# Fused attention and two-layer MoE kernel: the eight one-head products of each weight pair kept together, in a batch's last eight steps

## The chip, the cores and the metric

The kernel runs on one core of one Trainium2 chip. The metric is the device time in microseconds of one execution; lower is better. Inputs and output are float32.

## What is computed

Three stages follow one another, for 8 batches of 576 tokens and 8 heads of 64 columns.

```python
def sm_attn(qq, kk, vv):
    s = scale * np.matmul(qq, kk.transpose(0, 1, 3, 2))
    a = softmax(s)                       # per row
    return np.matmul(a, vv)
p_packed = sm_attn(p, k, v)              # 32 packed rows per batch and head ("pp")
out = sm_attn(q, p_packed, p_packed)     # attention of 576 tokens to 32 rows
x = out.transpose(0, 2, 1, 3).reshape(B * S, H * D)
h = x @ w_in                             # 512 -> 2048
x = (s * np.maximum(h, 0) ** 2 + b) @ w_out
a, b = x @ w1, x @ w2
return (a * b @ w3) @ w_out2
```

## The kernel before, in words

The kernel never forms the attention output. Since `x @ w_in` is (weights of the second softmax) times (pp w_in), it computes for each batch and head the 32 by 512 products **pp w_in** and multiplies them with the 256 by 576 softmax weights `AT` of the batch. Most products run in three passes of a high and a low part (`mm3`, lines 85 to 90): low weights by high data, high by low, high by high.

The work up to about 91 us (the first phase) computes pp of the first four batches (units of four heads: `A_tr`, `B_s1`, `C_tr`, `D_mm`, `D_ev`), decodes `w_in` from 64-bit words into `winx`, stores it to DRAM as `win_d`, and starts decoding `w_out`. The second phase is a loop over 256 steps (line 989 on): 8 batches by 2 halves of 288 tokens by 16 blocks of 128 columns of `w_in`. Step `idx` runs `step_h(idx + 3)` (6 products into `hps`: pp w_in by `AT`), whose result goes through ReLU and squares on ScalarE (ACT) and VectorE (DVE) to `gh` and `gl`, and `step_x(idx)` (12 products into the four banks `xps`: `w_out` by `gh`, `gl`). Beside them, by step numbers written in tables, run: the token tiles of a coming batch (`plan_q`: transpose `qtp`, scores `scp`, softmax, transpose `atp`; five per batch), the remaining units of pp (`plan`, which puts them into steps with room in the two banks of tag `a2`), the weight pairs described next, and decoding of later weights. The last phase (from about 900 us) is the second MoE.

**A weight pair** (`W_pair`, lines 498 to 518) makes pp w_in for two heads of an even batch and two of the odd batch after it, 512 columns wide. It is eight products (two heads `i`, two batches `bb`, two row halves `r`) of a 64-row by 32-column weight, each in a place of its own in the 128 by 128 array. The four with `bb = 0` fill one PSUM bank, `ps[0]`, the other four the second, `ps[1]`. Bank 0 is then read by an ACT cast (`wph`) and a DVE subtraction (`wpl`, which needs `wph`), bank 1 by an ACT copy (`wpst`). Both banks are the two buffers of tag `a2`, which token tiles and units also use. Their name in the profile is `wps`.

There are 32 pairs. The eight of batches 0 and 1 run in the first phase, in other banks. The other 24 run in the second phase, eight during each of batches 1, 3 and 5, for the two batches that follow. Their steps within the batch are `WAT`, those of the loads of their two pieces of `win_d` are `WLD` (two DMAs of 256 KB each into a ring of six buffers `wl`, so three pairs fit):

```python
WAT = (19, 20, 24, 25, 27, 28, 30, 31)
WLD = (13, 14, 16, 20, 21, 25, 26, 28)
```

Two pairs give the weights of four steps `step_h` of the next batch. All DMAs are issued by SyncE's queue (SP) in one order.

The order on each engine is not that of the code alone: a scheduler places an instruction when it expects its inputs to be ready, except where `tc.keep_in_program_order` holds those marked to the order of the code among themselves. The products of `W_pair` are marked in the first phase alone, and there those of bank 1 alone (`if bp == 0 and bb`).

Of the kernel before, what the change touches and what calls it, by code (L numbers as in the profile page):

```python
# [22 lines left out]
def fused_kernel(  # L23
# [24 lines left out]
    nc = tc.nc  # L48
    B, H, S, D = q.shape
    NP = p.shape[2]  # L50
# [13 lines left out]
    FB1 = F1 // P  # L64
# [55 lines left out]
    ppT = ppp.tile([P, NBP, NPAIR, 2, 2 * NP], F32, tag="ppT", name="ppT", bufs=1)  # L120
# [44 lines left out]
    if True:  # L165
# [332 lines left out]
        def W_pair(bp, j, ps, src):  # L498

            fc, c = divmod(j, 2)  # L500
            for i in range(2):
                for bb in range(2):
                    for r in range(2):
                        rows = slice(D * r, D * (r + 1))
                        o = NP * (r ^ bb)
                        h = 64 * (i ^ bb) + o
                        ins = nc.tensor.matmul(  # L507
                            ps[bb][h:h + NP], ppT[rows, bp, 2 * c + i, bb, o:o + NP], src[i][rows],
                            start=True, stop=True,
                        )  # L510
                        if bp == 0 and bb:
                            tc.keep_in_program_order(ins)
            if c == 0:
                wch[2 * bp, fc] = wch_tiles()
                wst[2 * bp + 1, fc] = wch_p.tile([P, 2, FC], F32, tag="wpst", name="wpst", bufs=4)
            hi, lo = wch[2 * bp, fc]
            split(hi[:, c], lo[:, c], ps[0])
            nc.scalar.copy(wst[2 * bp + 1, fc][:, c], ps[1])
# [8 lines left out]
        wd, wx = {}, {}  # L527
# [33 lines left out]
        ps = ps0.tile([P, 512], F32, tag="w", name="warm", bufs=2)  # L561
# [108 lines left out]
        ps = ps0.tile([P, 2, 512], F32, tag="s1", name="warm")[:, 0]  # L670
# [15 lines left out]
        def a2_ps(name):  # L686
            return psh.tile([P, 512], F32, tag="a2", name=name, bufs=2)
# [3 lines left out]
        def plan_q(b, j, o):  # L691

            def act(step, fn, first=False):
                l_ = qact.setdefault(step, [])
                l_.insert(0, fn) if first else l_.append(fn)

            qload.setdefault(max(o - 10, 0), []).append((b, j))
            act(o, lambda: q_tr(b, j, a2_ps("qtp")))
            act(o + 1, lambda: q_sc(b, j, a2_ps("scp")))
            act(o + 2, lambda: q_sm1(b, j))  # L700
            act(o + 3, lambda: q_sm2(b, j))
            act(o + 4, lambda: box.__setitem__((b, j), q_at(b, j, a2_ps("atp"))))
            act(o + 5, lambda: q_ev(b, j, box.pop((b, j))), True)
            a2use.update((o, o + 1, o + 4))
# [4 lines left out]
            plan_q(1, j, 12 + 5 * j)  # L709
        for b in range(2, B):  # L710
            for j in range(NTILE):
                plan_q(b, j, 2 * FB1 * (b - 1) + 2 + 5 * j)

        gt = {}

        def step_h(idx):
            b, f = divmod(idx, 2 * FB1)
            hf, f = divmod(f, FB1)
            fc, fo = divmod(f, FC // P)
            wh, wl = wch[b, fc]  # L720
            ah, al = AT[b, hf]
            ws = slice(fo * P, (fo + 1) * P)
            ps = psh.tile([P, 512], F32, tag="h", name="hps", bufs=2)
            for kc in range(2):
                mm3(ps[:, :HS], wh[:, kc, ws], wl[:, kc, ws],
                    ah[:, kc, :], al[:, kc, :], kc == 0, kc == 1)
            r = ap.tile([P, HS], F32, tag="r", name="r", bufs=3)
            nc.scalar.activation(r, ps[:, :HS], AF.Relu)  # L728
            gh = ap.tile([P, HS + 2], F32R, tag="gh", name="gh", bufs=4)
            gl = ap.tile([P, HS + 2], F32R, tag="gl", name="gl", bufs=4)  # L730
            if idx < FB1:
                nc.gpsimd.memset(gh[:, HS:].bitcast(F32), 1.0)
                nc.gpsimd.memset(gl[:, HS:].bitcast(F32), 0.0)
            by_act = idx % 2 or idx < FB1
            if by_act:
                nc.scalar.activation(gh[:, :HS], r, AF.Square)
            nc.scalar.activation(r, r, AF.Square)  # L737
            if not by_act:
                nc.vector.tensor_copy(gh[:, :HS], r)
            nc.vector.tensor_tensor(  # L740
                out=gl[:, :HS], in0=r, in1=gh[:, :HS].bitcast(F32), op=ALU.subtract
            )
            gt[idx] = (gh, gl)
# [3 lines left out]
        def step_x(idx):  # L747
            n, r = divmod(idx, 2 * FB1)
            b = n
            hf, f = divmod(r, FB1)  # L750
            gh, gl = gt.pop(idx)
            w = HS + 2 if idx < FB1 else HS
            for ob in range(KD):
                if f == 0:
                    xps[ob] = psh.tile([P, 512], F32, tag=f"x{ob}", name="xps")
                os_ = slice(ob * P, (ob + 1) * P)
                mm3(xps[ob][:, :w], wo_t[f][:, 0, os_], wo_t[f][:, 1, os_],
                    gh[:, :w], gl[:, :w], f == 0, f == FB1 - 1)
            if f == FB1 - 1:
                st = ap.tile([P, KD, HS], F32, tag="xst", name="xst", bufs=1)  # L760
                for ob in range(KD):
                    bc = bcol[:, ob:ob + 1]
                    if idx < FB1:
                        nc.vector.tensor_scalar_mul(bc, xps[ob][:, HS:HS + 1], sb_b[:, 0:1])
                    if ob % 2 == 0:
                        nc.scalar.activation(
                            st[:, ob, :], xps[ob][:, :HS], AF.Identity, bias=bc, scale=sb_s[:, 0:1]
                        )
                    else:
                        nc.vector.tensor_scalar(  # L770
                            out=st[:, ob, :], in0=xps[ob][:, :HS], scalar1=sb_s[:, 0:1],
                            scalar2=bc, op0=ALU.mult, op1=ALU.add,
                        )
                nc.sync.dma_start(
                    out=x2_d[b][hf].rearrange("(o p) t -> p o t", p=P), in_=st
                )
# [72 lines left out]
        NST = B * 2 * FB1  # L849
        for idx in range(3):  # L850
            step_h(idx)
        WAT = (19, 20, 24, 25, 27, 28, 30, 31)
        WLD = (13, 14, 16, 20, 21, 25, 26, 28)
        JOB0 = 66
        PRE = NST - 24

# [141 lines left out]
        for idx in range(NST):  # L998
            n, r = divmod(idx, 2 * FB1)
            if idx + AHEAD < FB1:  # L1000
                wo_dec(idx + AHEAD)
            if idx + AHEAD + 4 < FB1:
                wo_load(idx + AHEAD + 4)
            if idx == LATE:
                ctxl.close()
                ctxl.enter_context(ExitStack())
                p3["S"] = ctxl.enter_context(pool("ss"))
            nn, k = divmod(idx, 2 * FB1)
            if nn % 2 == 1 and nn + 1 < B:
                for j in range(len(WAT)):  # L1010
                    if k == WLD[j]:
                        W_load(j)
                    if k == WAT[j]:
                        W_pair((nn + 1) // 2, j, [a2_ps("wps") for _ in range(2)], wx.pop(j))
            nn, k = divmod(idx - 20, 2 * FB1)
            if nn >= 0 and nn % 2 == 0 and k in (0, 4, 8, 12):
                split_wp(nn + 1, k // 4)
            for fn in qact.pop(idx, ()):
                fn()
            for bj in qload.pop(idx, ()):  # L1020
                if bj[0]:
                    load_q(*bj)
            for fn in late.pop(idx, ()):
                fn()
            if idx >= JOB0:
                n, ph = divmod(idx - JOB0, 4)
                if ph and later:
                    later.pop(0)()
                if ph == 0:
                    job(n, 0)  # L1030
                    job(n - 2, 3)
                elif ph == 2:
                    job(n - 1, 1)
                elif ph == 3:
                    job(n - 1, 2)
            if idx + 3 < NST:
                step_h(idx + 3)
            step_x(idx)
            if PRE <= idx < PRE + 2 * FB2 and (idx - PRE) % 2 == 0:
                load_wo2((idx - PRE) // 2)  # L1040
            if PRE + 3 <= idx < PRE + 3 + 2 * FB2 and (idx - PRE) % 2 == 1:
                split_wo2((idx - PRE - 3) // 2)
            if idx in (NST - 12, NST - 8):
                load_w3(VM[(idx - NST + 12) // 4])
            if idx == NST - 3:
                V_tr(VM[0], a2_ps)
# [307 lines left out]
        j = NB3 - 1  # L1354
# [71 lines left out]
```

## Time and profile before

| | |
|---|---|
| time, three runs | 1446.88, 1448.70, 1449.66 us (median 1448.7) |
| profiled execution: time / span | 1446.5 / 1444.7 us |
| PE (TensorE) busy | 1424.6 us, 99% of the span |
| DVE / ACT busy | 851.2 us, 59% / 701.1 us, 49% |
| chain that ended last | 94% PE |
| all pairs' products: `wps` | 512 records, of 256 products |

The span is 1.8 us shorter than the execution's own time. A float32 product stands in the trace as two records (two passes), so a pair's eight products are 16 records, and one bank's four are 8. Products overlap, so their durations don't add up: what a group costs is read from the starts of its neighbours.

### The profile page before, as it was taken

What the parts mean: (1) busy time and instruction counts of PE and PEld (TensorE: products, weight loads), DVE (VectorE), ACT (ScalarE), POOL (GpSimd) and SP (SyncE); (2) the same over time, 40 slices, a digit from 0 to 9 for tenths busy, and PEclk for the clock granted to TensorE, in tenths of its full rate; (3) what the DMA queues carried; (4) which work ended last, traced back from release to release, by engine and by line L of the source; (5) the groups of instructions that cost most, each with busy time, mean ns of one, the idle gap of its engine ahead of it and who ended that gap; (6) DMA issues with size and microseconds to landing.
All of it is one profiled execution on the core that took longest, in us unless ns stands there. A gap on an engine that the chain in (4) does not pass through costs nothing.

```text
span 1444.7 us, 29157 instructions
## 1 busy us (share of the span) xinstructions
PE 1424.6 (99%) x11545; PEld 1314.6 (91%) x11545; DVE 851.2 (59%) x1686; ACT 701.1 (49%) x1509; POOL 4.2 (0%) x40
## 2 busy tenths in 40 slices
PE   8999999999999999999999999999999999999997
PEld 6569999699997799987999998999999999999997
DVE  5877544345644456665687337476685766757556
ACT  4777555455565556555676434142242433324323
POOL 0000000000000000000000000000000000000000
PEclk9999999999999999999999999999999999999999
DMA  8974220242433543445544143776675856757551
GB/s 287 342 276 136 64 65 26 94 141 66 147 110 102 188 122 112 124 157 166 160 163 154 55 143 111 237 237 180 191 232 156 264 164 196 226 165 215 160 162 44
DMA packets 177575, 228.93 MB, mean 158 GB/s; under 512 B 55584, under 2 KB 109856, under 8 KB 177440
## 3 DMA queue, kind: packets, MB, share of 16 engines
q1 hardware_dynamic: 177440, 227.08, 51.6%
q8 instruction: 92, 1.51, 0.4%
q14 instruction: 43, 0.35, 0.1%
HBM read 182.98 MB, written 44.04 MB: 157 GB/s over the span
## 4 chain that ended last, share of the span: by engine, by line
PE 94%; DMA 2%; DVE 2%; ACT 1%; issue 0%; SPq 0%; ACTq 0%
PE xps L89 10%; PE xps L90 10%; PE xps L86 10%; PE prod L86 8%; PE prod L90 7%; PE prod L89 7%; PE hps L86 5%; PE hps L90 5%; PE hps L89 5%; PE yps L89 4%; PE yps L90 4%; PE yps L86 4%; PE wps L507 3%; PE scp L201 2%; PE qtp L187 1%; PE w4a L86 1%
## 5 line engine op out<-in xcount | busy, mean ns | idle before, releaser
L89 PE MATMUL xps<-gl,wo 128*128 128x288 f32 (+1 forms) x1024 | 305.4, 299 | 0.0
L90 PE MATMUL xps<-gh,wo 128*128 128x288 f32 (+1 forms) x1024 | 304.8, 299 | 0.0
L86 PE MATMUL xps<-gh,wo 128*128 128x288 f32 (+1 forms) x1024 | 302.3, 299 | 0.0
L86 PE MATMUL prod<-xc,whl 128*128 128x384 f32 x672 | 226.3, 337 | 2.8 <-ACT Ta L1066 1.8
L90 PE MATMUL prod<-xc,whl 128*128 128x384 f32 x672 | 225.0, 335 | 0.0
L89 PE MATMUL prod<-xc,whl 128*128 128x384 f32 x672 | 224.9, 335 | 0.0
L86 PEld LDWEIGHTS xps<-gh,wo 128*128 128x128 f32 x1024 | 191.7, 188 | 10.4 <-issue 9.3
L90 PEld LDWEIGHTS xps<-gh,wo 128*128 128x128 f32 x1024 | 192.5, 188 | 9.4 <-issue 8.9
L89 PEld LDWEIGHTS xps<-gl,wo 128*128 128x128 f32 x1024 | 192.7, 188 | 8.3 <-issue 7.3
L740 DVE TENSOR_TENSOR gl<-r,gh 128x288 fp32r<-128x288 f32 x256 | 116.4, 455 | 126.7 <-ACT r L737 122.7
L728 ACT ACTIVATE r<-hps 128x288 f32<-128x288 f32 x256 | 105.2, 411 | 156.6 <-PE hps L90 155.0
L86 PE MATMUL hps<-ATh,wpl 128*128 128x288 f32 x512 | 154.5, 302 | 0.0
L89 PE MATMUL hps<-ATl,wph 128*128 128x288 f32 x512 | 152.8, 298 | 0.0
L90 PE MATMUL hps<-ATh,wph 128*128 128x288 f32 x512 | 152.3, 298 | 0.0
L1066 ACT COPY Ta<-prod 128x384 f32<-128x384 f32 x96 | 46.1, 480 | 215.5 <-PE prod L90 214.7
L90 PE MATMUL yps<-w4c,op 128*128 128x256 f32 x504 | 142.2, 282 | 0.0
L89 PE MATMUL yps<-w4c,op 128*128 128x256 f32 x504 | 142.1, 282 | 0.0
L86 PE MATMUL yps<-w4c,op 128*128 128x256 f32 x504 | 140.9, 280 | 0.0
L86 PEld LDWEIGHTS prod<-xc,whl 128*128 128x128 f32 x672 | 126.2, 188 | 7.3 <-ACT Ta L1066 3.8
L89 PEld LDWEIGHTS prod<-xc,whl 128*128 128x128 f32 x672 | 126.2, 188 | 0.0
L90 PEld LDWEIGHTS prod<-xc,whl 128*128 128x128 f32 x672 | 126.1, 188 | 0.0
L737 ACT ACTIVATE r<-r 128x288 f32<-128x288 f32 x256 | 112.8, 444 | 5.6
(161 smaller groups left out, 2378.5 us busy)
## 6 DMA issues: line engine op xcount, KB each, us to landing
whl<-whl SPq DMA_DIRECT2D x336, 256.0 KB, 3.1
raw<-in_moe_w_dram SPq DMA_DIRECT2D x32, 512.0 KB, 4.5
raw<-in_moe_w_out_dram SPq DMA_DIRECT2D x24, 512.0 KB, 4.4
wl<-win SPq DMA_DIRECT2D x48, 256.0 KB, 3.1
q<-in_q_dram SPq DMA_DIRECT2D x72, 128.0 KB, 3.6
x<-xst SPq DMA_DIRECT2D x16, 576.0 KB, 3.3
out_dram<-O SPq DMA_DIRECT2D x72, 128.0 KB, 2.4
raw<-in_moe_w_in_dram SPq DMA_DIRECT2D x16, 512.0 KB, 6.1
```

The source lines that it names most:

```text
L86: ins = nc.tensor.matmul(ps, wl, xh, start=start, stop=False, **kw)
L89: nc.tensor.matmul(ps, wh, xl, start=False, stop=False, **kw)
L90: nc.tensor.matmul(ps, wh, xh, start=False, stop=stop, **kw)
L187: nc.tensor.transpose(ps[:, pr * P:pr * P + n], src[:n, 2 * pr:2 * pr + 2, :].rearrange("p h d -> p (h d)"), ident[:n, :n],)
L201: nc.tensor.matmul(ps[sl, c:c + 64], qT[b, t][:, pr, sl], ppT[:, b // 2, pr, b % 2, :], start=True, stop=True,)
L507: ins = nc.tensor.matmul(ps[bb][h:h + NP], ppT[rows, bp, 2 * c + i, bb, o:o + NP], src[i][rows], start=True, stop=True,)
L728: nc.scalar.activation(r, ps[:, :HS], AF.Relu)
L737: nc.scalar.activation(r, r, AF.Square)
L740: nc.vector.tensor_tensor(out=gl[:, :HS], in0=r, in1=gh[:, :HS].bitcast(F32), op=ALU.subtract)
L1066: tc.keep_in_program_order(nc.scalar.copy(out, src))
```

## The change

In `W_pair` all eight products are marked to keep their order, bank 0's four before bank 1's, and ahead of them stands a new product of the same weight and data as the last of the eight, two columns wide, into bank 1 (the eight write over it). Pairs stand in steps 24 to 31 of the batch, after `step_h` of their step; their loads move to later steps; and the token tiles of batches 2, 4 and 6 stand every four steps instead of every five.

```diff
         def W_pair(bp, j, ps, src):
             fc, c = divmod(j, 2)
-            for i in range(2):
-                for bb in range(2):
+            ins = nc.tensor.matmul(
+                ps[1][:NP, :2], ppT[D:, bp, 2 * c + 1, 1, :NP], src[1][D:, :2], start=True, stop=True
+            )
+            tc.keep_in_program_order(ins)
+            for bb in range(2):
+                for i in range(2):
                     for r in range(2):
...
-                        if bp == 0 and bb:
-                            tc.keep_in_program_order(ins)
+                        tc.keep_in_program_order(ins)
...
-                plan_q(b, j, 2 * FB1 * (b - 1) + 2 + 5 * j)
+                plan_q(b, j, 2 * FB1 * (b - 1) + 2 + (4 if b % 2 == 0 else 5) * j)
...
-        WAT = (19, 20, 24, 25, 27, 28, 30, 31)
-        WLD = (13, 14, 16, 20, 21, 25, 26, 28)
+        WAT = (24, 25, 26, 27, 28, 29, 30, 31)
+        WLD = (20, 21, 22, 25, 26, 27, 28, 29)
...
-                    if k == WAT[j]:
-                        W_pair((nn + 1) // 2, j, [a2_ps("wps") for _ in range(2)], wx.pop(j))
...
             if idx + 3 < NST:
                 step_h(idx + 3)
+            for nn in range(1, B - 1, 2):
+                j = idx - 2 * FB1 * nn
+                if j in WAT:
+                    j = WAT.index(j)
+                    W_pair((nn + 1) // 2, j, [a2_ps("wps") for _ in range(2)], wx.pop(j))
             step_x(idx)
```

Three places show how the order on PE moves. A row is an instruction, or several alike; `32x512` is the output, and `[waits ...]` names the semaphores that it waits for (`DMAHW` a load, `Activation` ACT). First, PE near the end of batch 1, before: the sixth of the eight pairs.

```order
L89 MATMUL hps<-ATl,wph 128x288
L90 MATMUL hps<-ATh,wph 128x288
L507 MATMUL wps<-wl,ppT 32x512 [waits DMAHW4_49,DVE_49]
L507 MATMUL wps<-wl,ppT 32x512
L507 MATMUL wps<-wl,ppT 32x512 [waits DMAHW5_49]
L507 MATMUL wps<-wl,ppT 32x512
L86 MATMUL hps<-ATh,wpl 128x288
L89 MATMUL hps<-ATl,wph 128x288
L507 MATMUL wps<-wl,ppT 32x512 [waits Activation_49]
L507 MATMUL wps<-wl,ppT 32x512 x3
L90 MATMUL hps<-ATh,wph 128x288
```

The sixth pair of the same batch in the changed kernel:

```order
L86 MATMUL xps<-gh,wo_1485 128x288
L89 MATMUL xps<-gl,wo_1485 128x288
L90 MATMUL xps<-gh,wo_1485 128x288
L501 MATMUL wps<-wl,ppT 32x2 [waits DMAHW3_49,DVE_49]
L511 MATMUL wps<-wl,ppT 32x512 [waits DMAHW2_49,Activation_49]
L511 MATMUL wps<-wl,ppT 32x512 x7
L86 MATMUL hps<-ATh,wpl 128x288 [waits Activation_49]
L89 MATMUL hps<-ATl,wph 128x288
```

Four products, two of `hps`, four products have become the two-column product and eight in a row. Over the second phase the pairs stood in 44 separate groups (40 of four products, 4 of eight) and now stand in 24 groups of eight; in 18 of them the two-column product stands directly ahead of the eight, in 6 it stands alone among `xps` or `hps` products.

Second, PE at the change from batch 1 to batch 2 in the changed kernel: the second and third pair.

```order
L511 MATMUL wps<-wl,ppT 32x512 x7
L501 MATMUL wps<-wl,ppT 32x2 [waits DVE_49]
L86 MATMUL hps<-ATh,wpl 128x288
L89 MATMUL hps<-ATl,wph 128x288 [waits Activation_49]
L90 MATMUL hps<-ATh,wph 128x288
L86 MATMUL hps<-ATh,wpl 128x288
L89 MATMUL hps<-ATl,wph 128x288
L90 MATMUL hps<-ATh,wph 128x288
L511 MATMUL wps<-wl,ppT 32x512 [waits Activation_49]
L511 MATMUL wps<-wl,ppT 32x512 x7
```

The third pair's two-column product now stands right behind the second pair's eight, and the eight of the third six products later. In this batch the first pair stands in the 64th of the 256 steps of `xps`, the last in the 71st; before, they stood from the 54th to the 66th.

Third, PE a little earlier in the changed kernel: the two-column product of the first pair of batch 1.

```order
L483 MATMUL ppp<-swap,pvx 128x128 [waits DVE_49]
L90 MATMUL xps<-gh,wo_1935 128x288
L86 MATMUL xps<-gh,wo_1935 128x288
L501 MATMUL wps<-wl,ppT 32x2 [waits DVE_49]
L89 MATMUL xps<-gl,wo_1935 128x288
L90 MATMUL xps<-gh,wo_1935 128x288
```

It stands alone, 20 products ahead of its eight.

## Rows read from the trace of the kernel before

**Rows 1.** Page, part 1: busy time of each engine

```profile
PE 1424.6 (99%) x11545; PEld 1314.6 (91%) x11545; DVE 851.2 (59%) x1686; ACT 701.1 (49%) x1509; POOL 4.2 (0%) x40
```

**Rows 2.** Waits of PE from 240 to 700 us: total, times, longest

```profile
PE atp L235 <- DVE wpl L81: 0.3, 1, 0.3
```

**Rows 3.** Timeline of PE, half a pair (start, duration, line, tiles, records)

```profile
252.75 0.29 PE L86 MATMUL hps<-ATh,wpl 128*128 128x288 f32 x1
...
253.42 0.29 PE L90 MATMUL xps<-gh,wo 128*128 128x288 f32 x1
253.64 1.06 PE L507 MATMUL wps<-wl,ppT 64*32 64x512 f32 x8
254.63 0.40 PE L86 MATMUL xps<-gh,wo 128*128 128x288 f32 x1
254.87 0.29 PE L89 MATMUL xps<-gl,wo 128*128 128x288 f32 x1
```

**Rows 4.** Timeline of PE, first half pair of phase two, behind a token tile's scores

```profile
249.17 0.69 PE L201 MATMUL scp<-ppT,qT 128*64 128x64 f32 x16
249.78 1.06 PE L507 MATMUL wps<-wl,ppT 64*32 64x512 f32 x8
250.77 0.40 PE L89 MATMUL xps<-gl,wo 128*128 128x288 f32 x1
251.01 0.29 PE L90 MATMUL xps<-gh,wo 128*128 128x288 f32 x1
```

**Rows 5.** Timeline of PE, last half pair

```profile
683.81 1.06 PE L507 MATMUL wps<-wl,ppT 64*32 64x512 f32 x8
```

**Rows 6.** Timeline of PE, a pair whose eight products stood together

```profile
291.81 0.29 PE L90 MATMUL hps<-ATh,wph 128*128 128x288 f32 x1
292.04 1.09 PE L507 MATMUL wps<-wl,ppT 64*32 64x512 f32 x16
293.05 0.40 PE L86 MATMUL hps<-ATh,wpl 128*128 128x288 f32 x1
293.30 0.29 PE L89 MATMUL hps<-ATl,wph 128*128 128x288 f32 x1
```

**Rows 7.** Timeline of PE, a token tile's scores

```profile
97.16 0.69 PE L201 MATMUL scp<-ppT,qT 128*64 128x64 f32 x16
97.77 0.40 PE L89 MATMUL xps<-gl,wo 128*128 128x290 f32 x1
```

**Rows 8.** Timeline of PE, a single product of a pair in the first phase

```profile
59.23 1.04 PE L507 MATMUL wps<-winx,ppT 64*32 64x512 f32 x2
60.20 0.44 PE L235 MATMUL atp<-ident,E 128*128 128x128 f32 x2
```

**Rows 9.** Timelines of PE, ACT and DVE, a pair and its evictions

```profile
296.43 1.09 PE L507 MATMUL wps<-wl,ppT 64*32 64x512 f32 x16
...
297.62 0.59 ACT L78 CAST wph<-wps 128x512 fp32r<-128x512 f32 x1 [0.99 <-PE wps L507]
298.10 0.59 ACT L518 COPY wpst<-wps 128x512 f32<-128x512 f32 x1
...
298.24 0.69 DVE L81 TENSOR_TENSOR wpl<-wps,wph 128x512 fp32r<-128x512 f32 x1 [0.77 <-ACT wph L78]
```

**Rows 10.** Windows, pairs of batch 5: us, PE, PEld, DVE, ACT, POOL, PEclk, DMA, GB/s

```profile
639.00:691.00 52.00, 52.00 (x386) 36.29 (x387) 31.75 (x72) 30.82 (x67) 0.00 (x0) 1.00 0.53 161
```

**Rows 11.** Chain that ended last, 74 to 92 us: start, us, what

```profile
76.13 6.67 DMA raw<-in_moe_w_out_dram
...
82.81 4.17 DMA wl<-win
...
90.75 0.46 PE ppp L483 x2
```

**Rows 12.** Waits of SyncE's queue: total, times, longest

```profile
SPq L847 <- PE wps L507: 99.0, 18, 20.3
```

**Rows 13.** Page, part 6: the loads of the pairs, count, size, us to landing

```profile
wl<-win SPq DMA_DIRECT2D x48, 256.0 KB, 3.1
```

More of the change, by code (lines that the diff above doesn't have):

```diff
@@ L1007, in fused_kernel @@
                 p3["S"] = ctxl.enter_context(pool("ss"))
-            nn, k = divmod(idx, 2 * FB1)
-            if nn % 2 == 1 and nn + 1 < B:
+            for nn in range(1, B - 1, 2):
                 for j in range(len(WAT)):
+                    k = idx - 2 * FB1 * nn
                     if k == WLD[j]:
                         W_load(j)
-                    if k == WAT[j]:
-                        W_pair((nn + 1) // 2, j, [a2_ps("wps") for _ in range(2)], wx.pop(j))
             nn, k = divmod(idx - 20, 2 * FB1)
@@ L1037, in fused_kernel @@
                 step_h(idx + 3)
+            for nn in range(1, B - 1, 2):
+                j = idx - 2 * FB1 * nn
+                if j in WAT:
+                    j = WAT.index(j)
+                    W_pair((nn + 1) // 2, j, [a2_ps("wps") for _ in range(2)], wx.pop(j))
             step_x(idx)
```

## The prediction, made before the changed kernel was run

> **What bounds the kernel now.** I read the page first: PE is busy for 1424.6 of 1444.7 us [rows 1], and the chain that ended last is 94% PE. Then the waits of PE alone, in the stretch where the 24 moved pairs lie: from 240 to 700 us it waited once, for 0.3 us [rows 2]. So there the time is the sum of what PE's instructions take in their order, and nothing that only shortens a wait elsewhere can help. What the busy share hides stands in the timeline: products of a pair hold up the stream around them. In steady work a 128-row product starts every 0.134 us (five starts from 252.75 to 253.42, [rows 3]). A group of four products of a pair (8 records) starts 0.22 us after the last product before it, the next product starts 0.99 us later, and the one after that 0.24 us later [rows 3]: 1.45 us where two starts would take 0.27, so **1.18 us for half a pair**. When all eight stood together (16 records), the same three steps took 0.23, 1.01 and 0.25 us [rows 6]: 1.49 less 0.27, **1.22 us for a whole pair**. Second, and less visible, is that the price does not depend on the number of products: one alone held the array 0.97 us [rows 8], four 0.99, eight 1.01. Eight products in eight places run side by side, so breaking a pair in two buys a second fixed price.
>
> **What merging saves.** In the second phase of before there are 40 groups of four and 4 of eight, the first half pair at 249.78 [rows 4], the last at 683.81 [rows 5]. Of the 40, 36 stand among 128-row products: 36 x 1.18 = 42.5 us. Four stand right behind a token tile's scores. Scores end 0.61 us after their start with or without a pair behind them [rows 4, 7], so the way in is shared, and such a half adds 0.99 us: 4.0 us. The 4 whole ones add 4 x 1.22 = 4.9. Together 51.4 us. The changed order has 24 groups of eight, none beside scores: 24 x 1.22 = 29.3 us. **The gross gain is 22.1 us.**
>
> **What the two-column product costs.** No row shows it. In 18 groups it stands directly ahead of the eight, in the same array shape. Below, it is free, as one product took no less than eight. Above, it costs two records as dense as those of scores: 16 records in 0.61 us [rows 7], in two halves of the array, 8 behind each other, so 0.076 us each and 0.15 for two. The first passes of its neighbours go to other places, so I take 0.1: 1.8 us (0 to 2.7). In 6 groups it stands alone among 128-row products and adds a change of shape in and out. Below: the two edges of rows 3, 0.22 + 0.24 - 0.27 = 0.19, and two records, 0.34. Above: a whole tile of scores, 0.61 + 0.19 = 0.80. It is far nearer the first; I take 0.4: 2.4 us (2.0 to 4.8). So 17.9 us remain.
>
> **The new waits.** Before, each half waited for one bank. Now the two-column product waits for one bank, at the head of PE's queue, and the eight for the other; behind them stands everything. When is the second bank free? With a pair starting at 296.43, the cast runs at 297.62, the copy at 298.10, the subtraction from 298.24 to 298.93 [rows 9]: 2.50 us after the start. PE itself is through after 1.02 us. In the order shown with the change, most pairs have 14 or more products between them, so PE comes again after 1.02 + 0.24 + 13 x 0.134 = 3.0 us at the earliest, and does not wait. Three gaps of batches 1 and 3 are shorter. The third pair of batch 1 stands directly behind the second: 2.50 - 1.02 = 1.5 us. The second stands 9 products behind the first: 1.02 + 0.24 + 8 x 0.134 = 2.3, so 0.2 us. Batch 3 has 12 products in one gap: 2.7, no wait. I take **1.7 us of new waits**; from 0 (the weights of step 64 of `hps` wait for the same evictions anyway, but other work could have covered it) to 5 (every gap of batches 1, 3 and 5 at a batch's end late by 1 us, as ACT and DVE, busy 59% and 61% of the densest such stretch [rows 10], have other work ahead of an eviction).
>
> **Loads, tiles and queues.** The 48 loads are the same. Three pairs fit the ring, so loads of the fourth pair on wait for the pair three ahead, and SyncE's queue stands behind them: 99.0 us in 18 waits before [rows 12]. The loads now go out closer to their use, so I expect less of that. A load lands 3.1 us after its issue [rows 13], two steps take over 5 us (36 products at 0.134 and a pair or two), so it is there in time. What waits behind them in the queue, token tiles and the units' k and v, is used a few steps later. I cost this at nothing; without that cover a late load costs at most its own 3.1 us less the way to it. Tiles every four steps change no count: scores, transposes and unit products are as many, and groups of other shapes differ by one or two (within 0.5 us either way). POOL has nothing there.
>
> **The first phase.** Its eight pairs also close up, but I cost that at nothing. Its end hangs on DMA and decoding: the chain runs from 76.13 through a load of `w_out` and a store of `win` to 86.98, then through ACT and DVE to a product at 90.75 [rows 11]. PE time saved before that only waits longer. If that cover were thinner the gain is at most about 3 us; a worse order on DVE may cost 2.
>
> **The sum.** 22.1 - 1.8 - 2.4 - 1.7 = 16.2 us. The profiled execution took 1446.5 us, so 1430.3; the median of three lies 2.2 above it, so **1432 us** (1448.7 - 16.2 = 1432.5). With all bounds at their best, 22.1 - 2.0 + 3 = 23.1 gain: 1426. At their worst, 22.1 - 2.7 - 4.8 - 5 - 2 - 0.5 = 7.1: 1442.
>
> **The rivals.**
> Rival A, PE gains in the first phase too. For it: PE is nearly full there as well. Against: rows 11. 3 us more: 1429.
> Rival B, the evictions are late at the batch ends and half of the gain turns into waits at PE's head. For it: `hps` of the next batch needs the first two pairs, which now come ten steps later, in the 64th step instead of the 54th; in the order shown, `xps` of batch 1 run out there. Against: the 2.50 us. 8 us of wait: 1440.
> Rival C, slower: PE runs ahead of ACT, so that every one of the 24 pairs finds its bank taken. Such a wait per pair eats the gain at 17.9 / 24 = 0.75 us, and is slower by over 2.9 us from 0.87 us on. It decides where ACT's cast stands behind a ReLU whose `hps` products stand after the pair: one step (3.6 us) later the bank is free at 6.1 us, while PE, with 24 products between, comes at 4.3; 1.8 x 24 = 43 us less 18: 1474. For it: ACT works strictly in the order it was given. Against: in rows 9 ACT stood idle for 0.99 us waiting for the pair.
> Rival D, that merged products do not run side by side, since two of a bank's four come from the lower rows of the array and two from the upper, into one bank. If they took turns, a pair would hold PE twice 0.99, and 24 pairs would cost 24 x 2.2 = 53 us: no gain, with the two-column products about 1454. Against: rows 3 and 6 show such groups at 0.99 and 1.01. The Trainium skill (TensorEngine Tiling (Array Packing), Restrictions and Gotchas) says that different row tiles cannot access the same PSUM bank simultaneously, which would be this case; the 1.01 us row speaks against it. The change could also fail to do what it says, but on PE's own order the eight stand together in all 24 pairs.
>
> **How the numbers follow.** I give the forecast 0.74, A 0.10, B 0.08, C 0.05, D 0.03. A measurement of this kernel can tell about 0.2% (2.9 us) from no change. The forecast, A and nearly all of B are faster by over 0.2%: 0.90. A part of B and C where the waits just cancel the gain gives 0.04 for within 0.2%; the rest of C and D 0.06 for slower. The range is 1425 to 1442: it holds the forecast with its bounds, A, and B; what it leaves out is C, D and surprises.
>
> **What would show it.** Right: in the second phase `wps` in 24 groups, each 18 records (16 where the two-column product stands apart), the next product about 1.0 to 1.1 us after the start; batches 1, 3 and 5 each 5 to 6 us shorter, the other stretches unchanged; PE's waits of 1 to 2 us at the end of batch 1; phase one's end still near 91 us. Wrong: a pair that holds PE for 2 us (D); waits of PE for ACT or DVE evictions at most pairs (C) or of several us in one place (B); a wait of PE for `wl` loads.

## The result, and the profile after

| | before | changed |
|---|---|---|
| median of four runs each | 1448.99 us (1446.88 to 1449.66) | 1426.85 us (1425.45 to 1428.25) |
| profiled execution: time / span | 1446.5 / 1444.7 us | 1425.45 / 1423.3 us |

The ratio is 0.985, with a 95% interval of 0.9833 to 0.9867: 22.1 us less, where 16.2 were forecast. The time lies inside the range, near its low end.

The page's busy times, which answer to [rows 1]: PE is busy for 27 us less, VectorE (DVE) as long as before.

```profile
PE 1397.4 (98%) x11609; PEld 1312.4 (92%) x11609; DVE 851.3 (60%) x1686; ACT 696.9 (49%) x1509; POOL 3.9 (0%) x40
```

First, the second phase. The waits of PE from 240 to 700 us in the changed kernel (total, times, longest) answer to [rows 2], which had 0.3 us:

```profile
PE wps L501 <- DVE wpl L81: 1.4, 1, 1.4
PE wps L501 <- ACT wpst L521: 0.4, 1, 0.4
```

So PE is still the bound there. Its timeline (start, duration, line, tiles, records), at a pair with the two-column product (L501) directly ahead of the eight (L511), answers to [rows 6]:

```profile
286.32 0.29 PE L86 MATMUL xps<-gh,wo 128*128 128x288 f32 x1
286.55 0.19 PE L501 MATMUL wps<-wl,ppT 64*32 64x2 f32 x1
286.55 0.65 PE L511 MATMUL wps<-wl,ppT 64*32 64x512 f32 x7
286.60 0.17 PE L501 MATMUL wps<-wl,ppT 64*32 64x2 f32 x1
286.63 1.02 PE L511 MATMUL wps<-wl,ppT 64*32 64x512 f32 x9
287.58 0.40 PE L86 MATMUL hps<-ATh,wpl 128*128 128x288 f32 x1
287.82 0.30 PE L89 MATMUL hps<-ATl,wph 128*128 128x288 f32 x1
```

Eighteen records stand together, and the next product starts 1.03 us after the first of them; in [rows 6], with sixteen, it was 1.01. The first records of the eight start with those of the two-column product, not behind them, so it costs **0.02 us**. In the trace of the second phase 17 of the 24 pairs look like this.

Where the two-column product stands alone among 128-row products (the first pair of batch 1):

```profile
271.53 0.29 PE L86 MATMUL xps<-gh,wo 128*128 128x288 f32 x1
271.75 0.22 PE L501 MATMUL wps<-wl,ppT 64*32 64x2 f32 x2
271.90 0.40 PE L89 MATMUL xps<-gl,wo 128*128 128x288 f32 x1
272.14 0.29 PE L90 MATMUL xps<-gh,wo 128*128 128x288 f32 x1
```

The three steps take 0.22, 0.15 and 0.24 us: 0.61, less the 0.27 of two starts, **0.34 us**. At the change from batch 1 to batch 2, the second pair, with the third pair's two-column product directly behind it:

```profile
278.16 0.29 PE L90 MATMUL hps<-ATh,wph 128*128 128x288 f32 x1
278.38 1.09 PE L511 MATMUL wps<-wl,ppT 64*32 64x512 f32 x16
280.88 0.22 PE L501 MATMUL wps<-wl,ppT 64*32 64x2 f32 x2 [1.41 <-DVE wpl L81]
281.03 0.40 PE L86 MATMUL hps<-ATh,wpl 128*128 128x288 f32 x1
```

And what it waits for, on ACT and DVE (in brackets the engine's idle time before, and what ended it):

```profile
279.51 0.59 ACT L78 CAST wph<-wps 128x512 fp32r<-128x512 f32 x1 [2.05 <-PE wps L511]
279.99 0.59 ACT L521 COPY wpst<-wps 128x512 f32<-128x512 f32 x1
...
280.13 0.69 DVE L81 TENSOR_TENSOR wpl<-wps,wph 128x512 fp32r<-128x512 f32 x1 [1.97 <-ACT wph L78]
```

The bank is free 2.50 us after the pair's start, the same as in [rows 9], and the wait is **1.4 us**. One more, of 0.4, stands at the seventh pair of batch 5 (675.00). The pair before it started at 670.00 and 25 products stand between, but ACT had other work ahead of the evictions:

```profile
673.88 0.58 ACT L78 CAST wph<-wps 128x512 fp32r<-128x512 f32 x1
674.36 0.59 ACT L521 COPY wpst<-wps 128x512 f32<-128x512 f32 x1
```

So the bank came free 4.95 us after the pair's start there, and not 2.50. From the first `hps` product to the last `xps` the second phase took 756.5 us before (92.90 to 849.37) and takes 738.6 now (89.36 to 827.92): **17.9 us less**.

SyncE's queue stands less behind the pairs, as forecast (99.0 us in [rows 12]); the loads still land in 3.1 us, as in [rows 13]. Its waits:

```profile
SPq L850 <- PE wps L511: 75.3, 18, 23.6
```

Second, the first phase. Up to the third `ppp` product of a unit's end PE's order is the same in both kernels (585 records in the trace); behind it the eight pairs begin, in the old form ahead of the fourth `ppp` and in the new one after it. Before, the third starts at

```profile
51.03 0.49 PE L483 MATMUL ppp<-swap,pvx 128*128 128x128 f32 x2
```

and the eighth at 90.75 [rows 11], 39.7 us later; now they start at

```profile
49.57 0.49 PE L483 MATMUL ppp<-swap,pvx 128*128 128x128 f32 x2
...
87.19 0.49 PE L483 MATMUL ppp<-swap,pvx 128*128 128x128 f32 x2 [2.38 <-DVE pvx L472]
```

37.6 us apart: **2.1 us less**. The stretch also starts 1.5 us earlier, though the order up to there is the same; more on that below. 17.9 + 2.1 + 1.5 = 21.5, against 21.4 us by which the span is shorter.

The chain that ended last no longer runs through DMA there, as [rows 11] did, but through evictions of pairs and products (start, us, what):

```profile
75.38 0.48 ACT wph L78
75.86 0.50 ACT wpst L521
76.36 0.04 issue
76.40 0.33 PE ppp L485
76.73 0.12 PE wps L501
76.85 0.93 PE wps L511 x10
```

Windows of the stretch from the third to the eighth `ppp` product (us, PE, PEld, DVE, ACT, POOL, PEclk, DMA share, GB/s), before:

```profile
51.03:90.75 39.72, 36.73 (x750) 19.83 (x749) 31.90 (x80) 27.98 (x65) 0.38 (x8) 1.00 1.03 360
```

and in the changed kernel:

```profile
49.57:87.19 37.62, 31.47 (x767) 20.50 (x765) 32.57 (x81) 28.45 (x66) 0.38 (x8) 1.00 1.06 365
```

PE is 5.3 us less busy, and the stretch is 2.1 us shorter: the other 3.2 us have become waiting of PE. DVE, ACT and the DMA engines do much the same as before.

### The profile page after: what moved, and what is told of

It is laid out like the page before. It is cut to its first block, busy times and chain, and to the rows that moved or that the text cites. A ratio compares the mean times of both kernels' runs of the same rounds, so it can differ in the third digit from the quotient of the medians.

```text
span 1423.3 us, 29301 instructions
## 1 busy us (share of the span) xinstructions
PE 1397.4 (98%) x11609; PEld 1312.4 (92%) x11609; DVE 851.3 (60%) x1686; ACT 696.9 (49%) x1509; POOL 3.9 (0%) x40
## 4 chain that ended last, share of the span: by engine, by line
PE 89%; DMA 4%; DVE 2%; ACT 2%; SPq 1%; issue 1%; ACTq 0%; DVEq 0%
PE xps L86 9%; PE xps L90 9%; PE xps L89 9%; PE prod L86 8%; PE prod L90 7%; PE prod L89 7%; PE hps L86 5%; PE hps L90 5%; PE hps L89 5%; PE yps L89 4%; PE yps L90 4%; PE yps L86 4%; PE wps L511 2%; PE scp L201 2%; PE qtp L187 1%; DMA wo2st<-wo 1%
```

## The experiments

Two questions were open: whether the gain is that of the groups (theory 1, a fixed price for each change of shape), and where the gain in the first phase came from. Phase lengths below are read from each profile's timeline of PE, as above.

**The new pair alone**, with the old steps, loads and token tiles:

```diff
-        WAT = (24, 25, 26, 27, 28, 29, 30, 31)
-        WLD = (20, 21, 22, 25, 26, 27, 28, 29)
+        WAT = (19, 20, 24, 25, 27, 28, 30, 31)
+        WLD = (13, 14, 16, 20, 21, 25, 26, 28)
...
-                plan_q(b, j, 2 * FB1 * (b - 1) + 2 + (4 if b % 2 == 0 else 5) * j)
+                plan_q(b, j, 2 * FB1 * (b - 1) + 2 + 5 * j)
```

(the call of `W_pair` goes back to its old place too.)

> The changed W_pair alone, with the old steps, loads and tile spacing. In its order on PE the second phase has 24 groups of eight and 10 lone two-column products (6 in the change). Theory 1 (fixed price of a group): nearly the whole gain stays; 24 x 1.22 + 10 x 0.34 = 32.7 us of pairs against 51.4 before, and the first phase as in the change, so 1427 to 1430 us. Theory 2 (the place in the last eight steps is what matters, since only there both banks are free): PE waits for evictions at most pairs, and half or more of the gain is lost, 1438 us or more.

Measured 1427.56 us (1427.41 to 1428.35), ratio 0.9852 (0.9833 to 0.9871): the whole gain. The second phase took 739.4 us, against 738.6 in the change. Six of its ten lone two-column products stand behind a token tile's scores:

```profile
248.77 0.69 PE L201 MATMUL scp<-ppT,qT 128*64 128x64 f32 x16
249.39 0.22 PE L501 MATMUL wps<-wl,ppT 64*32 64x2 f32 x2
249.54 0.40 PE L89 MATMUL xps<-gl,wo 128*128 128x288 f32 x1
```

The scores take 0.62 us with it behind them as without [rows 7], so it adds 0.15 and no change of shape. Its waits of PE from 240 to 700 us are 2.2 us in all, near the change's 1.8, but at other places. The largest:

```profile
PE wps L511 <- ACT wpst L521: 1.7, 1, 1.7
```

So the new tables bring nothing measurable that the new pair does not bring alone.

**The new tables alone**, with the old pair: in `W_pair` the old loop and marks, steps, loads and tiles as in the change. Its second phase has 26 groups of four and 11 of eight.

> The new steps, loads and spacing with the old W_pair. Its order has 26 groups of four and 11 of eight in the second phase. Theory 1: 26 x 1.18 + 11 x 1.22 = 44.1 us, so 7 us less than before, no gain in the first phase: 1441 to 1443 us. Theory 2: most of the gain is here, under 1434 us.

Measured 1437.92 us (1435.46 to 1438.84), ratio 0.992 (0.9899 to 0.9941), somewhat more gain than expected. The second phase became 8.3 us shorter (748.2), and counting groups gives 51.4 - 26 x 1.18 - 11 x 1.22 = 7.3. Steps at the batch's end put more pairs whole into the order, and that is their gain. Of the rest of the 11.1 us by which the span is shorter, 1.8 had been won by the third `ppp` product (49.24 us), where the order is still that of before, so they are scatter.

**The marks without the two-column product**, in both phases:

```diff
-            ins = nc.tensor.matmul(
-                ps[1][:NP, :2], ppT[D:, bp, 2 * c + 1, 1, :NP], src[1][D:, :2], start=True, stop=True
-            )
-            tc.keep_in_program_order(ins)
```

> The change without the two-column product: the eight are still marked to keep their order. In PE's order of the second phase this gives the same groups as the old W_pair at the new steps, 26 of four and 11 of eight; in the first phase 7 of eight and 2 of four. Theory 1: 44.1 us of pairs, 7 us less than before, plus up to 3 from the first phase: 1439 to 1442 us. If marking the order alone keeps them together on the chip: 1427 us.

Measured 1436.57 us (1434.8 to 1438.87), ratio 0.9919 (0.9894 to 0.9944), somewhat less time than expected, and within the scatter of the tables alone. The second phase took 747.9 us, and the first phase's stretch 38.8, between the 39.7 of before and the 37.6 of the change. A bank's four still stand in a group of their own:

```profile
290.38 0.29 PE L90 MATMUL xps<-gh,wo 128*128 128x288 f32 x1
290.61 1.06 PE L507 MATMUL wps<-wl,ppT 64*32 64x512 f32 x8
291.60 0.40 PE L89 MATMUL xps<-gl,wo 128*128 128x288 f32 x1
```

Marks keep the order among the marked, and let others in between. It is the two-column product that makes the eight follow one another. That it does so by taking the wait for the second bank to the head is read from the order shown with the change, and the two-column product without the marks was not run.

**Four products instead of eight.** In the second phase the four products of the odd batch, their bank and the two-column product are left out:

```diff
-            for bb in range(2):
+            for bb in range(2 if bp == 0 else 1):
...
-            nc.scalar.copy(wst[2 * bp + 1, fc][:, c], ps[1])
+            nc.scalar.copy(wst[2 * bp + 1, fc][:, c], ps[1 if bp == 0 else 0])
```

> In the second phase the four products of the odd batch and the two-column product are left out, and the copy of the second bank reads the first: half of the pairs' products are not computed. Its order has 24 groups of four. Theory 1 (price of a group fixed, 1.18 for four and 1.22 for eight): 24 x 1.18 = 28.3 us against 24 x 1.22 + 6 x 0.34 + 0.4 = 31.7 in the change, and the 1.8 us of waits gone: 1421 to 1424 us. Rival (the price goes with the products): half of 29 us less, 1410 to 1413 us.

Measured 1423.21 us (1422.22 to 1425.57), ratio 0.9827 (0.9807 to 0.9847): half of the products gone, and 6 us less than the change on the same chip (1429.45, below). A group of four:

```profile
294.91 0.29 PE L90 MATMUL hps<-ATh,wph 128*128 128x288 f32 x1
295.14 1.06 PE L512 MATMUL wps<-wl,ppT 64*32 64x512 f32 x8
296.13 0.40 PE L86 MATMUL hps<-ATh,wpl 128*128 128x288 f32 x1
```

0.99 us for four, 1.01 and 1.03 for eight. The price belongs to the group. The second phase took 734.4 us, 6.0 less than in the change's profile on the same chip (740.5). The parts left out would make 7.0: 2.4 of two-column products, 24 x 0.04 of groups, and 3.6 of waits, which PE has from 95 to 830 us in that profile. Against the change's first profile, on another chip, it is 4.1 where the parts make 5.2. Either way counting is 1 us off.

**The second phase alone, the first phase alone.** The new pair is used only for batches from 2 on, with the new tables; or only for batches 0 and 1, with the old tables:

```diff
+            new = bp > 0
+            if new:
+                ...
+            for u in range(4):
+                bb, i = divmod(u, 2) if new else (u % 2, u // 2)
```

(`bp == 0` in the other.)

> The change in the second phase alone; the eight pairs of the first phase keep their old form. Theory 1 with a gain of the first phase of its own (about 3 us, as the traces of before and after have it): 1429 to 1431 us, first products of step 0 near 93 us. If the first phase only varies from run to run or ends by its loads as I forecast: 1427 us, as the change.

> The change in the first phase alone; steps, loads, spacing and the 24 later pairs as before. Gain of the first phase real: 1446 us, 2 to 3.5 below before, and the products of step 0 start near 89.5 us instead of 92.9. First phase bound by its loads (my forecast): 1449 us, within 1 us of before.

The first took 1431.24 us (1426.87 to 1436.06), ratio 0.9877 (0.9845 to 0.9909); its second phase, 740.3 us, is the change's. The second took 1445.69 us (1441.37 to 1446.69, ten runs), ratio 0.9975 (0.9963 to 0.9987): 3.6 us less than before, 1.9 to 5.4. Its second phase is that of before (757.0 us), and its stretch of the first phase took 37.8 us, against 39.7. So the first phase does gain. In the eight profiles with the new early pairs that stretch took 36.2 to 38.1 us, with the old ones 39.7 in the two where the clock did not fall. By the ratios the two parts add up, 17.8 + 3.6 = 21.4 us against 22.1, but the 17.8 may lie anywhere from 13.2 to 22.4.

The profile of the first of these two was also a lesson. Its time was the highest of its four (1436.06 us). Windows of its first phase, with the columns as above:

```profile
56.00:58.00 2.00, 2.00 (x53) 0.90 (x43) 1.97 (x9) 2.00 (x5) 0.10 (x1) 1.00 1.10 300
58.00:60.00 2.00, 0.43 (x12) 0.29 (x10) 2.00 (x6) 1.08 (x3) 0.00 (x0) 1.00 0.94 310
60.00:62.00 2.00, 0.57 (x6) 0.48 (x8) 1.28 (x4) 0.07 (x1) 0.00 (x0) 0.94 1.02 364
62.00:64.00 2.00, 2.00 (x25) 1.36 (x26) 0.00 (x0) 0.99 (x3) 0.00 (x0) 0.50 0.97 331
```

PE was nearly idle from 58 to 62 us, 3.0 of it in one wait of a `ppp` product for DVE, and then the granted clock fell to 0.50, the lower of its two levels (1.2 of 2.4 GHz). It was 0.81 on average from 54 to 72 us, and the eighth `ppp` came 6.6 us later than in [rows 11]. So the phases have to be compared one by one, never by the span alone.

The clock can also take back a part of the gain. In four of the eight profiles with the new early pairs it fell between the eighth `ppp` and the first `hps` product: here in the change on the other chip, and then in its first profile, where it did not.

```profile
89.16:92.64 3.48, 3.48 (x10) 2.77 (x11) 2.62 (x5) 1.55 (x4) 0.00 (x0) 0.59 1.03 411
87.19:89.36 2.17, 2.17 (x10) 1.83 (x11) 1.81 (x3) 0.49 (x3) 0.00 (x0) 1.00 1.03 413
```

The four lost 1.1 to 1.6 us by it. In the 4 us ahead PE was busy for 1.62 us in both of these, and for 2.44 in the kernel before; none of the four profiles without the new early pairs shows the fall there. What decides it no run shows.

**Every pair one step earlier**, to see whether the new waits can be had back:

```diff
-        WAT = (24, 25, 26, 27, 28, 29, 30, 31)
-        WLD = (20, 21, 22, 25, 26, 27, 28, 29)
+        WAT = (23, 24, 25, 26, 27, 28, 29, 30)
+        WLD = (19, 20, 21, 24, 25, 26, 27, 28)
```

> Pairs in steps 23 to 30, loads one step earlier; else the change. Same 24 groups and 6 lone two-column products. If the 1.4 us wait of the third pair of batch 1 comes from its place right behind the second: in this order a lone product and none directly behind an eight, so 1.4 us less, 1425 to 1426 us. If the end of batch 1 is bound by the a2 banks anyway: 1427 us, same.

> The change itself beside e5 to e7 on the same chip: 1426 to 1428 us.

Measured 1424.97 us (1422.65 to 1425.62) against 1429.45 (1424.09 to 1431.58) for the change, four runs each, with ranges that overlap. Both ran once more, on another chip:

> The same kernel as the earlier run with every pair one step earlier (steps 23 to 30), now with more runs, beside the change again. Theory 1 (a fixed price for each group, and the waits at the batch ends of 1.8 us in the change, 0.9 here): 1 us less than the change, which the runs can hardly resolve. Rival (the second phase's start and its waits vary from run to run by more than the step matters): no difference, medians within 1.5 us of each other, in either order.

> The change again, beside the kernel with its pairs one step earlier. Theory 1: 1426 to 1429 us, 1 us above that kernel. Rival: within 1.5 us of it, in either order.

1426.24 us (1423.95 to 1428.59), ratio 0.9843 (0.9818 to 0.9869), against 1428.52 (1427.85 to 1430.12), ratio 0.986 (0.9836 to 0.9884). Over both chips the kernel with earlier steps has a mean of 1425.4 us in 8 runs, the change 1428.7 in 9: 3.3 us less, with 2 either way by the scatter of the runs (2.7 with the change's first four runs beside them); on either chip alone the scatter is about as large as the difference. The rival (no difference) falls, and theory 1 forecast the side but a third of the size. Waits of PE from 95 to 830 us in this run of the change:

```profile
PE wps L501 <- DVE wpl L81: 1.4, 1, 1.4
PE xps L86 <- ACT xst L769: 1.0, 1, 1.0
PE wps L501 <- ACT wpst L521: 0.5, 1, 0.5
PE hps L86 <- ACT r L731: 0.4, 1, 0.4
```

With the earlier steps there are none in the same stretch, and its second phase is 3.1 us shorter (736.7 against 739.8): as much as these four add up to (3.3). On the first chip it was 737.6 us with 0.9 of waits, against 740.5 with 3.6. Those of L501 stand in every profile of the change; the other two do not stand in its first (738.6 with 1.8). With the earlier steps the second pair and the third's two-column product stand so:

```profile
277.24 0.19 PE L501 MATMUL wps<-wl,ppT 64*32 64x2 f32 x1
277.25 0.65 PE L511 MATMUL wps<-wl,ppT 64*32 64x512 f32 x7
...
279.94 0.22 PE L501 MATMUL wps<-wl,ppT 64*32 64x2 f32 x2
280.09 0.40 PE L86 MATMUL hps<-ATh,wpl 128*128 128x288 f32 x1
```

That leaves 2.70 us between them, where the bank needs 2.50. It is the fastest whole version here: faster than the kernel before by 1.6 to 1.7%, and than the change by about 0.2%.

## Why the prediction was right, and where its sum was off

**What bounds it, and the gross gain of 22.1 us: right.** PE is the sum of its instructions in the second phase, the fixed price of a group holds for four and for eight products, and 24 groups took the place of 44. 22.1 - 0.4 - 2.0 - 1.8 = 17.9 us is what the second phase lost in the trace. That it fits to the tenth is luck: the same counting was 1 us off with the tables alone and with four products.

**The two-column product next to the eight: mis-sized.** "I take 0.1: 1.8 us (0 to 2.7)". It measured 0.02, in all 0.4 us: the lower bound's reason (one product took no less than eight) was the right one, and the records of scores, to which the 0.1 leaned, were the wrong neighbour. The count of 18 is one too many: the third pair of batch 1 has its product behind the second's eight, where it took 0.15 us once it had its bank. **Alone: nearly right.** 0.34 us instead of 0.4, the lower bound, which was worked out from the edges of [rows 3].

**The new waits: right in the largest, by luck in the sum.** 1.8 us against 1.7, and the largest at the place and of the size that was named (1.4 against 1.5), by the same 2.50 us. The 0.2 forecast for the second pair of batch 1 did not come. In its place 0.4 stood in batch 5, behind evictions that were late by ACT's other work: that is the condition of rival C, at one pair. In the change's two later profiles the waits were 3.6 and 3.3.

**Loads, tiles and queues: right.** No wait of PE for a load of a pair, less standing of SyncE's queue.

**The first phase: this step failed.** "PE time saved before that only waits longer", since the chain of [rows 11] ran through DMA to 86.98. It was one chain among others that were nearly as late: PE was busy for 36.7 of the 39.7 us from the third `ppp` on. Of the 5.3 us of busy time saved, 3.2 did wait longer, but 2.1 shortened the phase in the change's profile, and 1.9 where only these pairs were changed. The chain now runs through evictions of pairs. In its place rival A holds, at 2.1 us by the trace instead of its 3; by the times of the run it is 1.9 to 5.4. What makes the gain there is open between two things: PE's shorter occupation, and evictions that can start earlier since a pair is complete sooner; no run separates them.

**By size:** the terms missed 1.4 (adjacent products) + 0.4 (alone) - 0.1 (waits) = 1.7 us, the first phase 2.1, and 1.5 us were the earlier start of that stretch. 16.2 + 5.3 = 21.5, against 21.4 in the spans and 21.05 in the profiled times. The start is scatter: in the twelve profiles here it lay from 49.2 to 52.0 us, while the order up to there does not depend on the change. So 1.5 us of the measured gain are luck of the two profiles.

**The rivals.** B (late evictions at several batch ends, 8 us of wait) fell: the waits are 1.8 us. C (every pair finds its bank taken) fell: two of 24 wait, one of them as C has it. D (the merged products take turns) fell by 1.03 us for eighteen records and by the run with four products. The Trainium skill (TensorEngine Tiling (Array Packing), Restrictions and Gotchas) says that different row tiles cannot access the same PSUM bank simultaneously. The trace does not agree with it for these shapes: two products from the lower rows and two from the upper, into one bank but on different partitions, took 0.99 us for four, against 0.97 for a single one [rows 8].

**One sign that was wrong:** batches 1, 3 and 5 were to be 5 to 6 us shorter each and the others unchanged. From one batch's last `xps` to the next one's, batch 1 went from 106.5 to 95.5 us and batch 2 from 93.4 to 99.9; from first to first, batch 1 went from 107.2 to 101.6 and batch 2 from 93.5 to 94.2. Now no `xps` starts from 276.93 to 284.72, while the pairs run there, so the batch's end is not where the saving can be read. Two batches together show it (4.5, 7.6 and 6.6 us).

## What to carry to other kernels

Where small products of another shape stand among large ones, count their groups, not their products: here a group cost 1.2 us whether it held four or eight, and a two-column product that takes the later wait to the head kept them together for 0.02 us, where marks of order alone did not. Then keep the groups further apart than their evictions take: here 2.5 us, and 4.95 where other work stood ahead of them. And before a saving beside a chain through DMA is costed at nothing, look how much later that chain is than the next one.

## What had not been expected of the hardware

The first records of eight 512-column products started in the same 0.05 us as a two-column product ahead of them, in the same array shape but in other places. The granted clock of the first phase hung on the run: in one profile PE waited for most of 4 us, the clock then went to 0.50, and the eighth `ppp` product came 6.6 us later, while in the others it was 1.00 from 54 to 72 us. At the phase's end it fell in four of eight profiles, to 0.54 to 0.63, after much the same 4 us of PE as in the others. Even where the order is the same, the third `ppp` product started anywhere from 49.2 to 52.0 us, more scatter than the second phase shows (738.6 to 740.5 us in three profiles of the change).
